# Routed attention and SwiGLU on one core: the third unit's additional cluster steps lose their weight in the spreading of pieces over gaps

## The chip, the cores and the metric

The kernel runs on one core of a Trainium2 chip. The metric is the device time of one execution in microseconds (us), as the median of several runs. The profiles are of single executions whose span is some 1.8 us shorter than the device time.

## The reference

Attention in which a query sees only the keys of its own cluster (the nearest of 16 centroids by cosine), 4 batches, 8 heads, 768 positions, 64 channels; then RMS norm and a gated feed-forward layer.

```python
q_assign = np.argmax(np.einsum('bhsd,hcd->bhsc', q_n, c_n), axis=-1)      # k_assign alike
mask = q_assign[:, :, :, None] == k_assign[:, :, None, :]
scores = np.where(mask, scale * np.matmul(q, k.transpose(0, 1, 3, 2)), -1e9)
attn = softmax(scores);  x = (attn @ v), heads side by side, 3072 x 512
xn = x / rms(x) * rms_g
out = (silu(xn @ w_gate) * (xn @ w_val)) @ w_out                           # 512 -> 1536 -> 512
```

## The kernel before

The program runs as eight units (u = 0 to 7), each half a batch's queries for all eight heads. A unit has 24 gaps, named (head, third). Each gap opens with two score matmuls and the exponential that follows on ScalarE; the value products of the head before come behind the second scores of each head. The rest of a gap is filled from a list of pieces: feed-forward work of the previous units, output matmuls, and transposes, casts and cluster steps of the group of heads that comes next. Each piece carries a weight, and `attention` spreads the list by it:

```python
def attention(heads, fill, skip=0, hooks={}):
    gaps = [(u, h, i) for u, h in heads for i in range(UNITS[u][2])]
    total, done, n = sum(c for c, _ in fill), 0.0, 0
    for at, (u, h, i) in enumerate(gaps):
        scores(u, h, i)                      # two matmuls on PE, one exponential on ScalarE
        ...                                  # pv of the head before, squares
        while n < len(fill) and at >= skip and done <= total * (at + 1 - skip) / (len(gaps) - skip):
            done += fill[n][0]
            fill[n][1]()
            n += 1
```

The orders of all engines follow from this list: an instruction that is issued earlier in the program stands earlier in its engine's queue. A gate piece and a value piece of the feed-forward layer, and a transposing piece, each take one of three PSUM buffers (`ps_g`, tag "gen") and give it back when another engine has read it:

```python
def gv(u, f, val):                           # gate piece (val=False), value piece (val=True)
    full = ps_g.tile([P, UQ], F32, tag="gen", ...)
    ...                                      # 4 matmuls
    ...                                      # the last unit's own branches are left out here
    if not val:
        nc.scalar.activation(th, ps, ACT.Tanh, scale=0.5)
        nc.vector.scalar_tensor_tensor(th, th, 1.0, ps, op0=ALU.add, op1=ALU.mult)        # reads gate: frees it
    else:
        nc.vector.scalar_tensor_tensor(gvT[u][:, f, :n], gates[u], 0.5, ps, ...)          # reads val: frees it

def trans(g, h, part, on=None):
    ps = ps_g.tile([P, UQ], F32, tag="gen", name="tq")
    ...                                      # 3 transposes on PE
    nc.scalar.activation(to, ps, ACT.Copy, scale=by)                                       # frees it
```

The third unit (u = 2) has five pieces that no later unit has: the second half of group 3's cluster steps, `a3[5:]`. Their weights are 0.7 (products, eight matmuls) and four times 0 (largest, compare, transpose back, place).

```python
fill = ffn_work(u - 2)[CUT:] + [(0.0, lambda u=u: rms(u - 1))]
fill += border(spread(o[:3], a3[5:]) + o[3:], ffn) if u == 2 else border(o, ffn)
attention([(u, h) for h in range(H)], fill + spread(ffn[CC:CUT], group(g) if g < NG else []), 1)
```

The softmax here doesn't subtract the row's maximum and nothing guards it: scores larger than these inputs give would overflow.

## Time and profile before

| | before |
|---|---|
| time, median of 3 runs | 347.0 us (346.91 to 347.26) |
| span of the profiled execution | 345.4 us |
| TensorE (PE) busy | 337.5 us, 98% |
| ScalarE, VectorE, GpSimd busy | 75%, 64%, 33% |
| granted TensorE clock | 1.0 |

PE is the bound. In a kernel like this the share of busy time says little more; what counts is where the matmul stream stands still. A gap's start can be read off the timeline as the start of its two score matmuls (L333), so the length of any stretch of gaps can be compared between units and between kernels to 0.01 us. That length is the difference of two starts, so a difference of 0.01 us between two lengths means nothing.

### The profile page before, as it was taken

To read this page: it belongs to the slowest core of one execution; us is meant where nothing else is said; L and a number is where in the kernel's file an instruction comes from. 1 tells how busy PE (TensorE), PEld (TensorE's weight loads), DVE (VectorE), ACT (ScalarE), POOL (GpSimd) and SP (SyncE) were. 2 spreads that over 40 slices of the span, in tenths; PEclk is the share of its full clock that TensorE was granted. 3 is DMA by queue.
4 is the path that set the end of the run, shared out by engine and by line. 5 is a ranking of instruction groups with operands and counts; after the bars stand their busy time and mean duration, and the time that the engine had idled before them with its cause. 6 is when DMAs were issued, how large, how long until landed. Compare 5 with 4: busy or idle time off the path is not lost.

```text
span 345.4 us, 7982 instructions
## 1 busy us (share of the span) xinstructions
PE 337.5 (98%) x3028; PEld 208.7 (60%) x3045; DVE 221.0 (64%) x540; ACT 259.5 (75%) x449; POOL 112.7 (33%) x225
## 2 busy tenths in 40 slices
PE   8999999999999999999999999999999999999996
PEld 4547657555665557655675656755566656665654
DVE  6999796975578636786367745686456644675330
ACT  5899979865878768887797877888778877764422
POOL 6999596234335304280132801535000000000000
DMA  7999989882450015401130011000100001001002
GB/s 265 392 203 197 264 165 235 140 273 90 140 166 15 12 61 169 139 20 37 61 94 2 23 47 46 2 8 18 63 32 0 2 33 61 2 1 64 30 2 91
DMA packets 27302, 31.62 MB, mean 92 GB/s; under 512 B 4480, under 2 KB 24320, under 8 KB 27264
## 3 DMA queue, kind: packets, MB, share of 16 engines
q1 hardware_dynamic: 18608, 25.02, 21.9%
q0 software_dynamic: 8368, 5.71, 10.2%
q8 instruction: 24, 0.39, 0.5%
q10 hardware_dynamic: 288, 0.39, 0.3%
q14 instruction: 14, 0.11, 0.1%
HBM read 28.35 MB, written 6.29 MB: 100 GB/s over the span
## 4 chain that ended last, share of the span: by engine, by line
PE 87%; ACT 6%; DVE 5%; issue 1%; POOL 0%; ACTq 0%; DVEq 0%; POOLq 0%
PE gate L423 17%; PE val L423 17%; PE o L448 17%; PE s L333 16%; PE acc L351 9%; PE tq L208 4%; ACT pT L337 4%; PE sc L241 3%; PE tx L396 1%; PE warm L117 1%; DVE pads L312 1%; DVE kext L317 1%; DVE qext L317 1%; PE o L459 1%; DVE scT L308 1%
## 5 line engine op out<-in xcount | busy, mean ns | idle before, releaser
L337 ACT ACTIVATE pT<-s,off 128x768 bf16<-128x768 f32 x192 | 170.6, 904 | 34.2 <-PE s L333 33.2
L333 PE MATMUL s<-qext,kext 80*128 80x384 bf16 x384 | 94.4, 327 | 1.9 <-ACT pT L337 1.1
L432 DVE SCALAR_TENSOR_TENSOR th<-th,gate 128x384 f32<-128x384 f32 x84 | 46.3, 552 | 52.1 <-ACT th L431 51.9
L423 PE MATMUL gate<-xnT,wg 128*128 128x384 bf16 x384 | 78.6, 325 | 0.5 <-DVE gvT L436 0.4
L423 PE MATMUL val<-xnT,wv 128*128 128x384 bf16 x384 | 78.1, 326 | 0.0
L448 PE MATMUL o<-wo,gvT 128*128 128x512 bf16 x259 | 66.0, 379 | 0.9
L227 POOL CAST qext<-qkT 64x384 bf16<-64x384 f32 x64 | 35.3, 557 | 76.4 <-PE acc L351 46.4
L333 PEld LDWEIGHTS <-kext 80*128 80x128 bf16 x384 | 36.5, 98 | 31.9 <-issue 7.0
L431 ACT ACTIVATE th<-gate 128x384 f32<-128x384 f32 x84 | 41.2, 490 | 14.2 <-PE gate L423 13.8
L423 PEld LDWEIGHTS <-wv 128*128 128x128 bf16 x384 | 36.1, 97 | 25.3 <-issue 3.8
L423 PEld LDWEIGHTS <-wg 128*128 128x128 bf16 x384 | 35.9, 97 | 25.1 <-issue 3.9
L436 DVE SCALAR_TENSOR_TENSOR gvT<-th,val 128x384 bf16<-128x384 f32 x84 | 46.2, 550 | 6.4 <-PE val L423 1.8
L351 PEld LDWEIGHTS <-pT 128*128 128x128 bf16 x1152 | 43.4, 97 | 10.1 <-DVE x L358 1.1
L351 PE MATMUL acc<-vbf,pT 128*128 128x65 bf16 x1152 | 45.7, 193 | 0.6 <-ACT pT L337 0.2
L448 PEld LDWEIGHTS <-gvT 128*128 128x128 bf16 x276 | 25.8, 97 | 25.1
L208 PE MATMUL tq<-ident_f,qk 128*128 128x128 f32 x192 | 31.2, 282 | 0.1
L214 ACT ACTIVATE qkT<-tq 128x384 f32<-128x384 f32 x57 | 26.9, 495 | 4.2 <-PE tq L208 3.7
L282 POOL DMA_DIRECT2D qext<-oh x40 | 19.1, 486 | 30.6 <-DVE oh L271 24.2
L397 DVE TENSOR_SCALAR xnT<-tx,gcol 128x384 bf16<-128x384 bf16 x28 | 10.6, 413 | 28.8 <-PE tx L396 28.8
L208 PEld LDWEIGHTS tq<-ident_f,qk 128*128 128x128 f32 x192 | 24.1, 145 | 6.8 <-ACT qkT L214 1.0
L451 ACT COPY o_sb<-o 128x512 f32<-128x512 f32 x23 | 13.5, 585 | 17.4 <-PE o L448 17.4
L282 POOL DMA_DIRECT2D kext<-oh x40 | 19.1, 485 | 9.6 <-DVE oh L271 9.6
(81 smaller groups left out, 247.7 us busy)
## 6 DMA issues: line engine op xcount, KB each, us to landing
qk<-in_q_dram SPq DMA_DIRECT2D x32, 192.0 KB, 3.9
vs<-in_v_dram SPq DMA_DIRECT2D x32, 192.0 KB, 4.1
out_dram<-o_sb SPq DMA_DIRECT2D x23, 256.0 KB, 2.0
qk<-in_k_dram SPq DMA_DIRECT2D x30, 192.0 KB, 3.9
wg<-in_moe_w_gate_dram POOLq DMA_DIRECT2D x4, 384.0 KB, 7.4
wv<-in_moe_w_val_dram POOLq DMA_DIRECT2D x4, 384.0 KB, 9.6
wo<-in_moe_w_out_dram POOLq DMA_DIRECT2D x3, 512.0 KB, 7.7
qext<-oh POOLq DMA_DIRECT2D x40, 12.0 KB, 1.6
```

Source lines behind the costliest of these rows:

```text
L208: nc.tensor.transpose(ps[:, i * P:(i + 1) * P], qk[:, part, 2 * i:2 * i + 2].rearrange("p t d -> p (t d)"), ident_f)
L214: nc.scalar.activation(to, ps, ACT.Copy, scale=by)
L227: on.tensor_copy(to, of)
L282: on.dma_start(out=ext[D:D + NC, h, e * UQ:(e + 1) * UQ], in_=put[g, m][32 * h + e * NC:32 * h + (e + 1) * NC])
L333: nc.tensor.matmul(ps[:, j, :w] if nt == HT else flat[:, j * w:(j + 1) * w], lhsT=cols(kext[g % 4][:KR, hh], g, kc // HT, kc % HT * P, (kc ...
L337: nc.scalar.activation(pT[u, h][:, n * i:n * i + n, :w], of, ACT.Exp, bias=off, scale=scale * ZS)
L351: nc.tensor.matmul(acc[:, h % 2, t], lhsT=pT[u, h][:, kc, t * P:(t + 1) * P], rhs=vbf[g % 4][:, hh, kc % HT * 2 + kc // HT], start=kc == 0 ...
L423: nc.tensor.matmul(ps, lhsT=w[:, c, f * P:(f + 1) * P], rhs=xnT[u][:, c, :n], start=c == 0, stop=c == CC - 1)
L431: nc.scalar.activation(th, ps, ACT.Tanh, scale=0.5)
L432: nc.vector.scalar_tensor_tensor(th, th, 1.0, ps, op0=ALU.add, op1=ALU.mult)
L436: nc.vector.scalar_tensor_tensor(gvT[u][:, f, :n], gates[u], 0.5, ps, op0=ALU.mult, op1=ALU.mult)
L448: nc.tensor.matmul(outs[u], lhsT=gvT[u][:, f, t * P:(t + 1) * P], rhs=wo[:, f], start=f == 0, stop=f == FC - 1)
```

## The change

The intent is that the additional steps should take no room in the spreading: the other pieces are then given to gaps by the same measure as in the later units.

```diff
-            fill += border(spread(o[:3], a3[5:]) + o[3:], ffn) if u == 2 else border(o, ffn)
+            fill += border(spread(o[:3], [(0.0, f) for _, f in a3[5:]]) + o[3:], ffn) if u == 2 else border(o, ffn)
```

## The prediction

> **What bounds the kernel now.** I read the busy table and the waits of the page first, then the sums of busy time per stretch, then the timeline of the stretch that the diff touches.
>
> From the page:
>
> ```profile
> PE   337.5 (98%) x3028; PEld 208.7 (60%) x3045; DVE 221.0 (64%) x540; ACT 259.5 (75%) x449; POOL 112.7 (33%) x225
> ...
> PE 87%; ACT 6%; DVE 5%; issue 1%; POOL 0%; ACTq 0%; DVEq 0%; POOLq 0%
> ```
>
> The TensorE (PE) is busy 337.5 of 345.4 us, and 87% of the chain that ended last is its own work. The clock is granted in full. So the matmul stream is the time: only its holes, 7.9 us in all and mostly at the two ends of the program, can be won back by a change of order. The waits of PE, whole program:
>
> ```profile
> PE s L333 <- ACT pT L337: 1.1, 4, 0.3
> PE warm L117 <- POOL warm L111: 1.0, 1, 1.0
> PE s L333 <- DVE qext L317: 0.5, 1, 0.5
> PE gate L423 <- DVE gvT L436: 0.4, 1, 0.4
> ```
>
> One of these, the single "gate L423 <- DVE gvT", lies in the third unit. The eight units (u = 0 to 7) can be told apart in the timeline: a unit has 24 gaps, each opened by two score matmuls (L333), and 18 attention-times-value matmuls (L351) follow the second scores of each head. The third unit runs from about 66 to 108 us; its gap (1,2), that is head 1, third scores, opens at 73.45, gap (4,0) at 86.17, gap (5,2) at 95.98. In the fourth unit the same three gaps open at 116.14, 127.98 and 137.02, in the fifth (4,0) and (5,2) at 169.02 and 178.06.
>
> **The change part by part.** Nothing is added or removed. Each unit spreads a list of pieces over its gaps by weight: a piece is put into a gap while the weight already placed is at most total x (gap number) / 23. In the third unit alone five pieces of group 3's clusters (products, largest, compare, transpose back, place) are woven into the first three output pieces. The products weigh 0.7, the other four weigh 0 already. The diff makes the 0.7 a 0. The total before: 8 x 0.64 + 9 x 0.86 + 4 x 0.18 + 0.7 + 16 x 0.64 + 8 x 0.3 + 2 x 0.7 = 28.32; after: 27.62. The allowance per gap falls from 1.231 to 1.201, and all that comes after the products counts 0.7 less. The order of the pieces among themselves stays; what moves is where the scores and the softmax exponentials (and the value products behind them) fall between them.
>
> I worked the rule through by hand for all 24 gaps. Nothing moves before (1,2) or after (5,1). Two stretches move.
>
> First, (1,2) to (3,0): the second output piece moves up into (1,2), one cluster step group and the following output pieces each move up by one. (1,2) then holds output, products, output; (2,2) two outputs; (3,0) one.
>
> Second, (4,0) to (5,1). Before: (4,0) gate 0; (4,1) transpose, val 0, transpose; (4,2) gate 1, val 1; (5,0) two transposes, gate 2; (5,1) val 2, transpose, gate 3. After: (4,0) gate 0, transpose; (4,1) val 0, transpose, gate 1; (4,2) val 1, transpose; (5,0) transpose, gate 2, val 2; (5,1) transpose, gate 3.
>
> The second list is exactly what the units without the additional steps already do: their total is 27.62. So the kernel before holds its own experiment. Busy time by stretch, (4,0) to (5,2), of the third, fourth, fifth and sixth unit (columns: stretch, length, then busy time of each engine, clock, DMA):
>
> ```profile
> 86.17:95.98 9.81, 9.34 (x90) 6.53 (x89) 5.26 (x12) 7.93 (x14) 3.03 (x6) 1.00 0.44 135
> 127.98:137.02 9.04, 9.04 (x91) 6.57 (x90) 5.14 (x12) 8.05 (x14) 3.02 (x6) 1.00 0.45 141
> 169.02:178.06 9.04, 9.04 (x91) 6.58 (x90) 5.11 (x12) 8.05 (x14) 3.02 (x6) 1.00 0.36 119
> 210.06:219.09 9.03, 9.03 (x90) 6.58 (x89) 5.12 (x12) 8.04 (x14) 3.02 (x6) 1.00 0.08 31
> ```
>
> Same work (one matmul record more or less), same DMA load in the third and fourth unit, and 9.81 against 9.04 us. The third unit loses **0.77 us** there. Where, the timeline shows (start, duration, engine, line):
>
> ```profile
> 89.95 0.89 ACT L337 ACTIVATE pT<-s,off 128x768 bf16<-128x768 f32 x1
> 90.73 0.49 ACT L431 ACTIVATE th<-gate 128x384 f32<-128x384 f32 x1
> 91.25 0.55 DVE L432 SCALAR_TENSOR_TENSOR th<-th,gate 128x384 f32<-128x384 f32 x1 [0.60 <-ACT th L431]
> 91.84 0.36 DVE L227 CAST kext<-qkT 64x384 bf16<-64x384 f32 x1
> 91.86 0.31 PEld L208 LDWEIGHTS tq<-ident_f,qk 128*128 128x128 f32 x3 [0.29 <-DVE th L432]
> 92.23 0.55 DVE L436 SCALAR_TENSOR_TENSOR gvT<-th,val 128x384 bf16<-128x384 f32 x1
> 92.83 0.81 PE L423 MATMUL gate<-xnT,wg 128*128 128x384 bf16 x4 [0.42 <-DVE gvT L436]
> ```
>
> Gate 1 stands behind the scores of (4,2), so its tanh stands behind that gap's 0.89 us exponential on ScalarE. Tanh, the first VectorE step, a cast and the second VectorE step follow one after the other, until 92.78; only then do the PSUM buffers of gate 1 and val 1 come free. There are three such buffers, and the two transposes and gate 2 of gap (5,0) want them all. The six transposes start at 91.32 and would take 6 x 0.109 = 0.65 us (in gap (6,0) six took 0.65), so gate 2 could start at 91.97; it starts at 92.83. That is 0.86 us of hole, of which the record shows only 0.42 as idle, since the modelled matmul ends cover the rest. In the fourth unit gate 1 stands ahead of the scores; there the tanh goes before the exponential:
>
> ```profile
> 131.99 0.49 ACT L431 ACTIVATE th<-gate 128x384 f32<-128x384 f32 x1 [0.16 <-PE gate L423]
> 132.37 0.89 ACT L337 ACTIVATE pT<-s,off 128x768 bf16<-128x768 f32 x1
> ...
> 133.42 0.49 PE L208 MATMUL tq<-ident_f,qk 128*128 128x128 f32 x3
> ...
> 133.83 0.81 PE L423 MATMUL gate<-xnT,wg 128*128 128x384 bf16 x4
> ```
>
> The three transposes at 133.42 need 0.33 us and gate 2 follows after 0.41: a hole of 0.08. So 0.86 - 0.08 = 0.78 us, the 0.77 of the stretches.
>
> The first stretch has nothing to win:
>
> ```profile
> 73.45:86.17 12.72, 12.56 (x104) 6.72 (x106) 8.69 (x30) 7.42 (x10) 3.81 (x8) 1.00 0.52 182
> 116.14:127.98 11.84, 11.73 (x99) 6.63 (x98) 5.99 (x20) 8.10 (x16) 0.00 (x0) 1.00 0.12 46
> ```
>
> The third unit takes 12.72 - 11.84 = 0.88 us more than the fourth, and the cluster products that only it has take 0.78 us at 74.73 plus 0.09 us of start: 0.87. The new order there is again the fourth unit's with the products put in.
>
> PE is dense after (5,2) (12.16 of 12.16 us busy), so what is won should stay won. Sum: 0 - 0.77 + 0 = -0.77 us; 347.0 - 0.77 = **346.2 us**, 0.2%.
>
> **What the Trainium skill says.** "PSUM — Partial Sum Buffer", section Engine vs sequencer instructions: the queues of ScalarE and VectorE are strict FIFO, and matmuls start and complete in program order. The trace agrees: the tanh at 90.73 follows the exponential at 89.95 although gate 1 was done by 90.50. "Perfetto Trace Analysis", section Optimization Strategy: look for the gaps on the most contended engine and what releases them; repeated bubbles can mean too few buffers. Here it is one bubble, not a repeated one: the other units have it at 0.08 us. The same page, section Identifying the Most-Contended Engine, warns that matmul busy share overstates closeness to the limit; the trace agrees in small, with 0.86 us of hole recorded as 0.42.
>
> **The rivals.** (a) *No gain: the hole moves.* The PSUM buffers may be handed out differently; in the fourth unit gate 2 waits for a transposed tile's copy on ScalarE (ends 133.78), not for val 1's VectorE step (ends 134.04). If the third unit waits for the latter, 134.04 + 0.05 - 133.83 = 0.26 us come back: 346.5 us. Earlier products could also delay something on VectorE: the new order puts "largest" and "compare" ahead of a normalisation (L358), which would end about 1.1 us later, near 80.7, while the next value products want its accumulator at 82.9. Hidden, so no cost. (b) *A slower place.* The cluster rows go by eight DMA issues on GpSimd from 81.57 to 85.38, landing 1.6 us after each, and head 4's scores want the first of them at 86.17. The VectorE work ahead of it is the same sum, in another order, so it should start at the same time; if it came 1 us late, PE could wait up to about 1 us: 347.2 us. The first issues, which head 4 needs, land near 84, so I give it little. (c) *ScalarE becomes the bound* in the moved gaps: it is busy 8.05 of 9.04 us in the fourth unit's stretch, close, but PE loses nothing there. 346.2 us.
>
> **Range and chances.** Three runs spread from 346.91 to 347.26, so 0.35 us is the noise of one reading. The full gain gives 346.2, the partly returned one 346.5, none 347.0. Range 345.9 to 346.9. Two per cent are 6.9 us, nine times the whole effect: same 0.98, faster 0.01, slower 0.01.
>
> **What would show it.** Right: the third unit's (4,0) to (5,2) takes 9.0 to 9.1 us; "gate L423 <- DVE gvT" vanishes from the waits of PE; the tanh of gate 1 runs ahead of its neighbouring exponential; (1,2) to (4,0) stays at 12.7; the fourth unit's gaps come 0.8 us earlier and are otherwise the same. Wrong: a new wait for a PSUM release in (5,0), a wait of scores for the placed rows at (4,0), or a gain eaten in the units behind.

## The result

| | before | after |
|---|---|---|
| time, median of 4 runs each | 346.96 us (346.77 to 347.26) | 346.08 us (345.86 to 346.38) |
| span of the profiled execution | 345.4 us | 344.5 us |
| third unit, (1,2) to (4,0) | 12.72 us | 12.72 us |
| third unit, (4,0) to (5,2) | 9.81 us | 9.04 us |
| third unit, (5,2) to the next unit | 12.16 us | 12.16 us |

The ratio of the times is 0.9975 with a 95% interval of 0.9957 to 0.9992. Ratios here are the mean time of one kernel's fast runs over that of the other's of the same rounds, so not quite the ratio of the medians.

The busy table of the page after:

```profile
PE 337.7 (98%) x3045; PEld 208.4 (61%) x3045; DVE 220.4 (64%) x540; ACT 259.4 (75%) x449; POOL 112.8 (33%) x225
```

PE's busy time did not fall. (It rose by 0.2 us. This trace holds 17 more of the output matmuls' records, which probably accounts for it.) The gain is a hole that is gone. The busy time by stretch after, for the third unit's (1,2) to (4,0), (4,0) to (5,2) and (5,2) to its end, and the fourth unit's (4,0) to (5,2) (columns: stretch, length, then PE, weight loads, VectorE, ScalarE, GpSimd, clock, DMA share, GB/s):

```profile
73.31:86.03 12.72, 12.72 (x108) 6.70 (x106) 8.72 (x30) 7.22 (x10) 3.81 (x8) 1.00 0.51 179
86.03:95.07 9.04, 9.04 (x90) 6.57 (x89) 5.13 (x12) 8.04 (x14) 3.02 (x6) 1.00 0.46 145
95.07:107.23 12.16, 12.16 (x113) 7.29 (x111) 8.94 (x21) 9.88 (x20) 3.87 (x8) 1.00 0.37 111
127.07:136.11 9.04, 9.04 (x91) 6.58 (x90) 5.13 (x12) 8.05 (x14) 3.02 (x6) 1.00 0.46 140
```

The second line is the one that changed: 9.81 to 9.04 us. It now equals the fourth unit's, and nothing before or behind it moved. Laid gap by gap against the trace before, every score pair from the third unit's (5,2) to the end of the eighth unit comes 0.91 us earlier. Of that, 0.14 us is there from the first score pair at 10.5 us on, long before the change; over all the traces that start lies between 0.42 us earlier and 0.32 us later than in its base, so it is noise. The rest is 0.77 us.

The first three waits of PE, whole program, after:

```profile
PE s L333 <- ACT pT L337: 1.1, 4, 0.3
PE warm L117 <- POOL warm L111: 1.0, 1, 1.0
PE s L333 <- DVE qext L317: 0.4, 1, 0.4
```

The wait of a gate for VectorE's `gvT` is gone. The timeline of the third unit's (4,2) and (5,0), after, from the tanh of gate 1 to gate 2 (rows that don't bear on it are left out, here and in the timelines below):

```profile
90.04 0.49 ACT L431 ACTIVATE th<-gate 128x384 f32<-128x384 f32 x1 [0.16 <-PE gate L423]
90.43 0.89 ACT L337 ACTIVATE pT<-s,off 128x768 bf16<-128x768 f32 x1
...
91.35 0.49 ACT L214 ACTIVATE qkT<-tq 128x384 f32<-128x384 f32 x1
91.47 0.49 PE L208 MATMUL tq<-ident_f,qk 128*128 128x128 f32 x3
91.53 0.56 DVE L436 SCALAR_TENSOR_TENSOR gvT<-th,val 128x384 bf16<-128x384 f32 x1
...
91.89 0.81 PE L423 MATMUL gate<-xnT,wg 128*128 128x384 bf16 x4
```

The tanh runs ahead of the exponential, and gate 2 follows the transposes at 91.89. One thing here is easily missed: gate 2 starts at 91.89, before the VectorE step on val 1 has ended at 91.53 + 0.56 = 92.09. So it cannot be waiting for val 1's buffer. The copy of the transposed tile (L214) ends at 91.35 + 0.49 = 91.84, and the semaphore on which gate 2 waits in this trace is the one that ScalarE raises. In the kernel before, gate 2 waited for VectorE. The buffers are handed out differently.

### The profile page after: what moved, and what is told of

It reads as the page before. It is cut to its first block, busy times and chain, and to the rows that moved or that the text cites. A ratio compares the mean times of both kernels' runs of the same rounds, so it can differ in the third digit from the quotient of the medians.

```text
span 344.5 us, 7999 instructions
## 1 busy us (share of the span) xinstructions
PE 337.7 (98%) x3045; PEld 208.4 (61%) x3045; DVE 220.4 (64%) x540; ACT 259.4 (75%) x449; POOL 112.8 (33%) x225
## 4 chain that ended last, share of the span: by engine, by line
PE 88%; ACT 5%; DVE 5%; issue 1%; POOL 0%; ACTq 0%; DVEq 0%; POOLq 0%
PE gate L423 17%; PE val L423 17%; PE o L448 17%; PE s L333 16%; PE acc L351 9%; PE tq L208 4%; ACT pT L337 4%; PE sc L241 3%; PE tx L396 1%; PE warm L117 1%; DVE pads L312 1%; DVE kext L317 1%; DVE qext L317 1%; PE o L459 1%; DVE scT L308 1%
## 5 line engine op out<-in xcount | busy, mean ns | idle before, releaser
L448 PE MATMUL o<-wo,gvT 128*128 128x512 bf16 x276 | 67.6, 379 | 0.0
L214 ACT ACTIVATE qkT<-tq 128x384 f32<-128x384 f32 x57 | 26.9, 495 | 3.7 <-PE tq L208 3.2
```

What stands on the lines that cost most here:

```text
L448: nc.tensor.matmul(outs[u], lhsT=gvT[u][:, f, t * P:(t + 1) * P], rhs=wo[:, f], start=f == 0, stop=f == FC - 1)
```

## The experiments

The result agrees with the prediction's sum. Open was whether its reason is right: that the hole comes from the tanh standing behind the exponential. A rival had come up while the two traces were compared. Before, gate 1 is done only at 90.50 (89.69 + 0.81), and the exponential started at 89.95 and lasted 0.89 us, so it can delay the tanh by no more than the 0.23 us from 90.50 to 90.73. The 0.77 us would then be a sum of smaller terms.

For most experiments `attention` got a list of counts (`plan`) that says how many pieces are placed by the end of each of the third unit's 24 gaps. With the old list it issues the kernel before, with the new list the changed kernel.

```diff
-            while n < len(fill) and at >= skip and done <= total * (at + 1 - skip) / (len(gaps) - skip):
+            while n < len(fill) and (n < plan[at] if plan else at >= skip and done <= ...):
```

The lists, gap (0,0) to (7,2):

```
old: 0 2 4  6 8 11  12 18 19  21 24 27  28 31 35  38 43 45  50 53 56  61 63 66
new: 0 2 4  6 8 12  15 18 20  21 24 27  29 33 36  40 43 45  50 53 56  61 63 66
```

The stretch (4,0) to (5,2) of the third unit in all of them:

| kernel | (4,0) to (5,2) | against its base | time ratio to before (95%) |
|---|---|---|---|
| before | 9.81 us | | |
| after | 9.04 us | -0.77 | 0.9975 (0.9957 to 0.9992) |
| second_only | 9.04 us | -0.77 | 0.9984 (0.9967 to 1.0002) |
| first_only | 9.82 us | +0.01 | 0.9994 (0.9981 to 1.0006) |
| gate_ahead | 9.30 us | -0.51 | 0.9981 (0.9969 to 0.9993) |
| exp_behind | 9.63 us | -0.18 | 0.9995 (0.9984 to 1.0007) |
| transpose_ahead | 9.23 us | -0.58 | 0.9983 (0.9969 to 0.9998) |
| gate_and_transpose | 9.03 us | -0.78 | 0.9975 (0.9961 to 0.9990) |
| cast_behind | 9.50 us | -0.31 | 0.9991 (0.9978 to 1.0004) |
| lru_after (base: after) | 9.29 us | +0.25 | 1.0005 (0.9992 to 1.0018) |
| tanh_behind (base: after) | 9.94 us | +0.90 | 1.0006 (0.9992 to 1.0020) |

The intervals of the times are as wide as the effects, so they decide little; they agree in direction. In every one of these kernels the other stretches of the third unit kept their length within 0.01 us, (1,2) to (4,0) at 12.72 or 12.73 and (5,2) to the next unit at 12.16 us.

**second_only and first_only: which of the two moved stretches?** The lists were cut at gap (4,0).

```diff
+PLAN = old[:12] + new[12:]     # second_only
+PLAN = new[:12] + old[12:]     # first_only
```

> The kernel before with the pieces of the third unit given to its gaps by a fixed list: the old placing up to gap (3,2), the new one from (4,0) on. Theory (the whole gain sits in (4,0) to (5,1)): (4,0) to (5,2) falls from 9.81 to 9.04 us and everything behind comes 0.77 us earlier, as in the changed kernel. Rival (the earlier stretch, where the products and outputs move, has a share, or the gain is in the products' weight itself): clearly less than 0.77 us, down to 0.

> The other half: the new placing up to gap (3,2), the old one from (4,0) on. Theory: (4,0) to (5,2) stays at 9.81 us and nothing behind comes earlier (0.00 us, within 0.05, against the start of the third unit). Rival: some of the 0.77 us shows here.

Measured 9.04 and 9.82 us, and all gaps behind kept that difference. The whole gain is in (4,0) to (5,1); where the cluster products and the first outputs stand is worth nothing. The weight matters only because everything behind the products counts 0.7 less.

**gate_ahead and exp_behind: is it the exponential ahead of the tanh?** The first moves gate 1 ahead of the scores of (4,2), which is the new list's order for this piece. (A piece of casts that stands in front of it in the list goes along; in the trace the orders of VectorE and GpSimd are those of the kernel before.) The second leaves PE, VectorE and GpSimd in the old order and issues the exponential of (4,2) behind gate 1's tanh.

```diff
 # gate_ahead, gap (4,1)
-old[13] = 31
+old[13] = 33
 # exp_behind
-            scores(u, h, i)
+            held = scores(u, h, i, (u, h, i) == (2, 4, 2))     # returns the exponential unissued
...
                 fill[n][1]()
-                n += 1
+                n, _ = n + 1, held() if held and n == 32 else None     # piece 32 is gate 1
```

> The kernel before with one piece moved: gate 1 goes from behind the scores of (4,2) to ahead of them; transposes and val 1 stay. Theory as predicted (the tanh behind the exponential is the whole hole): tanh goes ahead of the exponential and the 0.77 us come back in full. Rival (the hole is a sum of three delays: about 0.2 us by the exponential, 0.33 us by the scores between, the rest by which PSUM buffer gate 2 gets): tanh at about 0.04 us after gate 1, val 1's VectorE step ends about 0.53 us earlier, gain about 0.5 us, 0.3 us of hole left.

> The kernel before with TensorE, VectorE and GpSimd orders untouched; only on ScalarE the exponential of (4,2) is issued behind gate 1's tanh. Theory as predicted (the exponential ahead of the tanh makes the hole): the hole closes, gain about 0.77 us. Rival (gate 1 is only done at 90.50, when 0.34 us of that exponential are left, so it delays the tanh by 0.23 us only): tanh at 90.54, gate 2 at about 92.64 instead of 92.83, gain 0.15 to 0.2 us.

The timeline of exp_behind, from gate 1 to gate 2:

```profile
89.56 0.81 PE L423 MATMUL gate<-xnT,wg 128*128 128x384 bf16 x4
90.41 0.49 ACT L431 ACTIVATE th<-gate 128x384 f32<-128x384 f32 x1 [0.49 <-PE gate L423]
90.80 1.69 ACT L337 ACTIVATE pT<-s,off 128x768 bf16<-128x768 f32 x2
90.93 0.55 DVE L432 SCALAR_TENSOR_TENSOR th<-th,gate 128x384 f32<-128x384 f32 x1 [0.41 <-ACT th L431]
91.91 0.56 DVE L436 SCALAR_TENSOR_TENSOR gvT<-th,val 128x384 bf16<-128x384 f32 x1
92.52 0.65 PE L423 MATMUL gate<-xnT,wg 128*128 128x384 bf16 x3 [0.42 <-DVE gvT L436]
```

With the exponential out of the way the tanh starts 0.85 us after gate 1's first matmul, that is 0.04 us after its last has ended, and still PE is recorded idle for 0.42 us before gate 2, on `gvT`. The stretch fell by 0.18 us and not by 0.77. The prediction's mechanism in its narrow form is refuted: the exponential explains about a quarter. Moving the gate itself gave 0.51 us. The order on PE, first of the kernel before, then of gate_ahead with its tanh and gate 2:

```profile
89.36 0.49 PE L333 MATMUL s<-qext,kext 80*128 80x384 bf16 x2
89.69 0.81 PE L423 MATMUL gate<-xnT,wg 128*128 128x384 bf16 x4
```

```profile
89.24 0.81 PE L423 MATMUL gate<-xnT,wg 128*128 128x384 bf16 x4
89.89 0.49 PE L333 MATMUL s<-qext,kext 80*128 80x384 bf16 x2
90.09 0.49 ACT L431 ACTIVATE th<-gate 128x384 f32<-128x384 f32 x1 [0.16 <-PE gate L423]
92.19 0.81 PE L423 MATMUL gate<-xnT,wg 128*128 128x384 bf16 x4 [0.18 <-DVE gvT L436]
```

Before, the two score matmuls (0.33 us, 89.36 to 89.69) stand ahead of gate 1. In gate_ahead they stand behind it, between gate 1 and val 1, so gate 1 itself starts earlier by 0.33 us. (My expectations for gate_ahead and gate_and_transpose have this the wrong way round where they speak of "scores between"; the size is right.) Counted from the start of (4,0), the VectorE step on val 1 ends at 6.61 us in the kernel before, 6.42 in exp_behind and 6.09 in gate_ahead: 0.19 us earlier without the exponential in the way, and 0.33 us more without the scores in front. That is the 0.18 + 0.33 = 0.51.

**transpose_ahead and gate_and_transpose: where are the last 0.26 us?** The first moves only the first transpose of (5,0) into (4,2), ahead of the scores of (5,0); the second moves it and gate 1.

```diff
-old[14] = 35
+old[14] = 36                    # transpose_ahead
+old[13], old[14] = 33, 36       # gate_and_transpose
```

> The kernel before with only the first transpose of (5,0) moved ahead of the scores of (5,0); gate 1 stays behind the scores of (4,2). Theory: the terms are not a plain sum. If gate 2 is given the transposed tile's buffer, it no longer waits for val 1's VectorE step and starts when the second transpose is through, itself held to 91.87 by gate 1's VectorE step: gate 2 at about 92.25, gain about 0.55 to 0.6 us. If gate 2 still gets val 1's buffer, the gain is 0.00 us.

> The kernel before with two pieces moved: gate 1 ahead of the scores of (4,2), and the first transpose of (5,0) ahead of the scores of (5,0). Theory now (three terms: exponential ahead of tanh 0.20 us and scores between gate 1 and val 1 0.33 us, as gate_ahead showed with 0.53 us, and a last 0.25 us because the transposed tile is copied ahead of the exponential of (5,0), so that its PSUM buffer is there for gate 2): the full 0.77 us. Rival (the last 0.25 us comes from the other pieces that the change moves: transposes of (4,0) and (4,1), val 2): stays at 0.5 us.

Measured 9.23 and 9.03 us. Two moved pieces give the whole gain; the other pieces that the change moves in this stretch (transposes of (4,0) and (4,1), val 2) give nothing measurable. The two moves are not a plain sum, 0.51 + 0.58 = 1.09 against 0.77 to be had, since they shorten two ways to the same start: gate 2 needs only the one buffer that it is given. In transpose_ahead:

```profile
91.71 0.49 ACT L214 ACTIVATE qkT<-tq 128x384 f32<-128x384 f32 x1 [0.29 <-PE tq L208]
...
92.06 0.55 PE L208 MATMUL tq<-ident_f,qk 128*128 128x128 f32 x3
...
92.42 0.56 DVE L436 SCALAR_TENSOR_TENSOR gvT<-th,val 128x384 bf16<-128x384 f32 x1
92.44 0.81 PE L423 MATMUL gate<-xnT,wg 128*128 128x384 bf16 x4
```

Here the VectorE step on val 1 only starts at 92.42, and gate 2 starts at 92.44 without waiting for it. The transposed tile's copy was done at 92.20, so its buffer was free, and gate 2 had only to let the second transpose pass. That one waited until 92.06 for gate 1's own VectorE step, which ends at 92.00: this is the 0.19 us that transpose_ahead lacks to the full gain.

**cast_behind: does the length of the VectorE chain set the hole before?** In the old order, the key cast between the two VectorE steps goes behind the second one.

```diff
+            fill[33:35] = fill[33:35][::-1] if u == 2 else fill[33:35]     # old list: cast <-> val 1
```

> The kernel before with one swap on VectorE: the key cast between gate 1's and val 1's steps goes behind val 1's step; all other engines in the old order. Theory (gate 2 waits for the end of the VectorE chain of gate 1 and val 1): val 1's step ends at 92.39 instead of 92.78, gate 2 starts about 0.38 us earlier. Rival (gate 2 waits for something else that ends near 92.8, such as the copy of the transposed tile at 92.86): 0.00 us.

Measured 9.50 us, 0.31 us less, where 0.38 was expected. The chain does set the hole before. The difference is in the trace: without the cast between them, the second VectorE step starts at 92.21, some 0.10 us after the first has ended at 91.55 + 0.56 = 92.11, where the cast before it had left only 0.03 us.

**lru_after: is it the choice of buffer?** The order of all engines is that of the changed kernel (compared row by row, no difference), but a rule of the kernel's own hands out the three buffers: the least recently used that is not open (in use by output matmuls that are still adding up). The edit is shortened here.

```diff
+    gen = lambda shape, dt, tag, name: (turn.append(turn.pop(next(j for j, k in enumerate(turn) if k not in kept))),
+                                        ps_g.tile(shape, dt, tag=f"gen{turn[-1]}", name=name, bufs=1))[1]
-    ps_g.tile(        # at every use
+    gen(
```

> The changed kernel with the same order on all engines, but the three PSUM buffers of the pieces handed out by a fixed rule: the one least recently used and not open. Theory (in the new order gate 2 starts early because it is given the transposed tile's buffer, free at 91.84, and not val 1's, free at 92.09): gate 2 of (5,0) starts about 0.25 us later in the third to sixth unit, together about 1.0 us slower than the changed kernel. Rival (the rule gives the same buffers, or the buffer plays no part): the same time as the changed kernel.

```profile
91.47 0.49 ACT L214 ACTIVATE qkT<-tq 128x384 f32<-128x384 f32 x1
91.60 0.49 PE L208 MATMUL tq<-ident_f,qk 128*128 128x128 f32 x3
91.66 0.56 DVE L436 SCALAR_TENSOR_TENSOR gvT<-th,val 128x384 bf16<-128x384 f32 x1
...
92.27 0.81 PE L423 MATMUL gate<-xnT,wg 128*128 128x384 bf16 x4 [0.18 <-DVE gvT L436]
```

Gate 2 now waits for val 1's step (91.66 + 0.56 = 92.22) although the transposed tile's buffer was free at 91.96. Against the changed kernel the gaps fall back by 0.27, 0.26, 0.26 and 0.26 us at (5,1) of the third, fourth, fifth and sixth unit. Between the start and there the rule cost nothing that lasts (0.11 us later at the first score pair, which is noise, and 0.12 in the third unit up to there). So 0.26 of the 0.77 us hangs on the buffer. In the kernel before, the third unit's gate 2 had been given val 1's buffer, in the changed kernel it is given the transposed tile's. Another choice alone would not have helped the kernel before: there the transposed tile's copy on ScalarE stood behind the exponential of (5,0) and ended at 92.86, after val 1's step at 92.78. It takes both, the transpose moved ahead of that gap's scores and its buffer given to gate 2. How the framework chooses was not studied; only that the choice differs between the two orders, and what it is worth.

**tanh_behind: the same swap on ScalarE in the new order.** Only the tanh of gate 1 goes behind the exponential of (4,2). The edit is shortened here.

```diff
-                nc.scalar.activation(th, ps, ACT.Tanh, scale=0.5)
-                nc.vector.scalar_tensor_tensor(th, th, 1.0, ps, op0=ALU.add, op1=ALU.mult)
+                later.append(lambda: (the two, unissued)); (u, f) == (1, 1) or later.pop()()
...
-            scores(u, h, i)
+            scores(u, h, i); later and later.pop()()
```

> The changed kernel with TensorE, VectorE and GpSimd orders untouched; only on ScalarE gate 1's tanh goes behind the exponential of (4,2). Theory (the order on ScalarE matters through the release of gate 1's buffer for the second transpose): exponential 90.43 to 91.33, tanh to 91.72, gate 1's VectorE step to 92.31, second transpose at 92.36 instead of 91.47, gate 2 at about 92.77 instead of 91.89: about 0.9 us slower than the changed kernel, as slow as the kernel before. Rival (the order on ScalarE is worth 0.20 us, as taking the exponential out of the way gained in the old order): 0.2 us slower than the changed kernel.

Measured 9.94 us for the stretch, 0.90 us more than in the changed kernel and more than in the kernel before. The size was as expected, the way was not. I had expected the second transpose to wait for gate 1's VectorE step; in the trace it waited for the transposed tile's copy on ScalarE, which the late tanh had pushed back, and later val 2 waited for VectorE. Here too the buffers had been handed out anew. The same pair of instructions on ScalarE, swapped, is thus worth 0.18 us in one order of PE and 0.90 us in the other.

**start_filled and start_filled_all: a version better than both?** In both kernels PE waits at the start of the eighth unit, where no piece stands between the first two score pairs. In start_filled the eighth unit may fill its first gap; in start_filled_all every unit from the third on may.

```diff
-            attention([...], fill + spread(...), 1)
+            attention([...], fill + spread(...), u < NU - 1)     # start_filled
+            attention([...], fill + spread(...), 0)              # start_filled_all
```

> The changed kernel, and beside it the last unit (u = 7) may place pieces into its first gap too. In both kernels PE stands there for 0.42 us, because the second scores wait for the last exponential of the sixth unit's end and nothing lies between. Theory: a gate of 0.65 us between the two score pairs covers the wait; 0.42 us faster than the changed kernel, if no other gap of that unit opens. Rival: the shift of all later pieces of the unit by a part of a gap opens another hole of the same size: no gain.

> As start_filled, but in all units from the third on (24 instead of 23 gaps share the weight). At each start of a unit PE stands 0.06 us before the second scores and 0.15 us before a value piece. Expected if each hole is local: up to 0.2 us more for each of five units, 1.4 us in all against the changed kernel. Rival: the gaps of (4,0) to (5,1) fall differently again and the 0.77 us hole, or a like one, comes back in each unit: slower by up to 3 us.

start_filled, waits of PE:

```profile
PE s L333 <- ACT pT L337: 0.8, 3, 0.3
```

One of the four waits for an exponential is gone. Laid against the changed kernel, the last score pair moves from 0.38 us earlier (the start's noise) to 0.79 us earlier within the eighth unit: a gain of 0.41 us, where 0.42 was expected. Its median is 346.04 us (345.42 to 346.33), its ratio to the kernel before 0.9970 (0.9956 to 0.9983). That beats the kernel before; that it beats the changed kernel is shown by the trace alone, for the two were not run in the same rounds and the intervals overlap.

start_filled_all is the miss: 348.03 us, ratio 1.0028 (1.0015 to 1.0042), slower than both. The wait at the start of each unit goes, but with 24 gaps the pieces fall differently and new holes open in each of the third to sixth unit, among them 0.25 us before gate 2 and 0.39 us before a value piece. Another shift of the spreading, and the same kind of hole.

## Why the prediction was right, and where not

- **The size and place.** The predicted 346.2 us against 346.08; (4,0) to (5,2) at 9.04 us as in the later units; the first stretch unchanged. The ground that carried this was the comparison of the third unit with its neighbours in the trace before, which does not depend on knowing why. second_only and first_only confirm it. That the hole before gate 2 (0.86 - 0.08 = 0.78) agreed with it was no test of the cause, since both measure the same hole.
- **The step that failed** is in "Where, the timeline shows": "Gate 1 stands behind the scores of (4,2), so its tanh stands behind that gap's 0.89 us exponential on ScalarE". The order is read rightly, but only a part of the hole is its consequence: exp_behind measured 0.18 us for it. The sum is: exponential ahead of the tanh 0.18 us, two score matmuls ahead of gate 1 0.33 us (together 0.51, gate_ahead), and 0.26 us for the first transpose of (5,0), copied before that gap's exponential (gate_and_transpose) so that gate 2 can be given its PSUM buffer (lru_after), 0.77 us in all. This is the sum in the order in which the pieces were moved; transpose_ahead alone, moved first, gave 0.58 us. The times for seeing this stood in the prediction's own lines: the exponential ends at 90.84, gate 1 at 90.50.
- **"only then do the PSUM buffers of gate 1 and val 1 come free"**, as the condition of gate 2, was right for val 1 in the kernel before (cast_behind), and wrong as a rule for the other orders: there gate 2 can take the transposed tile's buffer. For gate 1 it misreads its own lines: its VectorE step ends at 91.25 + 0.55 = 91.80, and the second transpose, which waited for it, goes on at 91.86. The 0.86 us are two waits one behind the other, some 0.28 us of the second transpose for gate 1's buffer and some 0.58 us of gate 2 for val 1's (the last matmul of the second transpose starts at 92.14 in the trace and would take 0.11).
- **Rival (a)**, another hand-out of buffers, was put at 0.26 us and a total of 346.5. It did not occur in the changed kernel; forced, it measured 0.26 us in each of four units.
- **Rival (b)**: the eight placing issues started at 81.46 and took 3.81 us, with no wait of the scores at (4,0). The normalisation behind "largest" and "compare" ended at 80.68, near the predicted 80.7, without cost. **Rival (c)**: ScalarE is busy 8.04 of 9.04 us there, and PE lost nothing.
- **"won should stay won"** held: the 0.77 us are the same at the end of the eighth unit.

## What to carry to other kernels

Where a program repeats a pattern and one repeat runs longer, measure the same stretch in the other repeats first: the difference is an estimate of the gain to be had, before any mechanism is known. Then test the mechanism with a swap on one engine alone, because the instruction that stands in front in a queue delays only by what is left of it when the next one is ready (here some 0.2 of 0.89 us). When work is interleaved by weights, a shift can also change who waits for which buffer, as it did here, so a change of a weight should be read from the stretches it moves and not from its intent.

## What the Trainium skill lacked or had wrong

- "Perfetto Trace Analysis", section Optimization Strategy: it says that repeated bubbles can mean too few buffers, and names no other cause of them. Here, with the same three PSUM buffers, the hole before the same gate piece measured 0.86 us before the change and 0.08 us after, by the order of pieces and the hand-out of buffers that comes with it. Nor does the page give a measure of how much of a PE hole goes unrecorded as idle because matmul ends are modelled: the longest record here is 0.42 us of the 0.86.
- "PSUM — Partial Sum Buffer", section Engine vs sequencer instructions: strict FIFO on ScalarE agrees with the traces here (the order swapped in the program of exp_behind and of tanh_behind is the order swapped in their traces, and nothing else on ScalarE). It gives no measure of what that costs; the same two ScalarE instructions swapped were worth 0.18 us in one order of the matmuls and 0.90 us in another.
- No page has what a different hand-out of PSUM buffers costs with all engine orders equal: 0.26 us for each of four units here.
